# Casting double-precision weights on the chip: the last bit from a rounded sum in ScalarE, and a new fixed order of the first batch

## The chip, the core and the metric

The kernel runs on one core of a Trainium2 chip. The core has five engines with a queue of instructions each: TensorE (PE, with its weight loads shown as PEld), VectorE (DVE), ScalarE (ACT), GpSimd (POOL), and SyncE (SP), which here issues the loads. Each queue is worked off in order; semaphores hold an instruction until what it needs is there. The metric is device time in microseconds (us), lower is better.

## The reference

Two blocks in a row. The first is a gated linear attention (4 batches, 8 heads, 768 tokens, 48 channels a head); the second takes its output as a 768 x 384 matrix for each batch, mixes it with a two-dimensional Fourier transform, normalises it, and sends it through two projections with a residual.

```python
f = 1.0 / (1.0 + np.exp(-f_logit))
for t in range(S):
    state = f[:, :, t, :, None] * state + np.einsum('bhd,bhe->bhde', k[:, :, t], v[:, :, t])
    y[:, :, t] = np.einsum('bhd,bhde->bhe', q[:, :, t], state)
...
x = y.transpose(0, 2, 1, 3).reshape(B, S, H * D)
u = x + np.real(np.fft.fft(np.fft.fft(x, axis=1), axis=2))
un = (u - mean(u)) / np.sqrt(var(u) + 1e-06)
out = u + np.maximum(un @ w_ch1, 0.0) @ w_ch2
```

The two weight matrices (384 x 1536 and 1536 x 384) come as 64-bit floats. The kernel turns them into 32-bit floats on the chip: 24 blocks of 128 x 384 values.

## The kernel before, in words

A **unit** is one pair of heads of one batch; there are 16, four for each batch, numbered 0 to 15. `attention` (with `outputs`) is a generator: each `yield` ends a stage of a unit. Its stages, by the tiles they write: the gate's logarithm in `g` (a clamp on DVE, two activations on ACT); its running sum by a scan on DVE (L188), then two exponentials on ACT into `W` and `g`; two products on DVE (`W`, `q`; L199, L200), behind which the loads of f and k for unit u + 3 are issued, into the same buffers; the scores `sc` on PE (L210), masked into `at` by DVE (L214); the transposed keys `st`, copied to `kT` by ACT; the state's updates `ds` on PE, chained by a DVE scan into `stt`; the outputs `y` on PE in two sets (L381, L388); `yT`; the transpose `yt`; and its copy into `x` on ACT. `fold` then adds and subtracts halves of `x` for the Fourier transform (`eo`, `xs`, `xc`).

`fnet` is the second block for one batch: three groups of matmuls `z` (L461) with copies `zz`; the matmuls `mix` (L474), added to `x` by DVE; mean and variance by DVE (`bs`, `mv`) and two small activations (`rstd`); then, for each half of the 768 tokens, the normalised rows `un` (DVE), their transposes `pt` (PE) and copies `unT` (ACT), 12 groups of `up` (L516, w_ch1, each copied to `h` by ACT with a Relu), and three groups of `po` (L528, w_ch2), each over 12 blocks of `w2`.

A weight block is converted by `single`. The 64-bit words land in `raw` (two buffers of 384 KB), as a low and a high word for each value. DVE builds the sign, exponent and mantissa from the high word (L151, L152) and the low one (L153), takes the bit to round by (L155), POOL adds it (L156), and DVE multiplies small values to zero (L157) by a size that ACT took (L149). `weights(n)` converts what is missing of the first n blocks, ahead of the matmul that reads them.

The order of the first batch is written out by hand: the block under `manual_schedule` calls `step(u)` (one stage of a unit), `fill()` (one stage of `fnet`) and `weights(n)`. The program then goes on in the loop behind it, and there a scheduler orders the instructions of each engine.

Of the kernel before, what the change touches and what calls it, by code (L numbers as in the profile page):

```python
# [16 lines left out]
SMALLEST = 1.125 * 2.0 ** -15  # L17
X_MIN = -24.0
# [3 lines left out]
def kernel(  # L22
# [30 lines left out]
    pr = ctx.enter_context(tc.tile_pool(name="pr", bufs=2))  # L53
    p3 = ctx.enter_context(tc.tile_pool(name="p3", bufs=4))
    ph1 = ctx.enter_context(tc.tile_pool(name="ph1", bufs=14))
# [24 lines left out]
    masks = fixed([128, 4, 32], "masks")  # L80
    ident = fixed([128, 128], "ident")
    eps = fixed([128, 1], "eps")

    place = const.tile([128, B, 3], U32, tag="place", name="place")
    nc.gpsimd.iota(place, pattern=[[S, B], [-C, 3]], base=S, channel_multiplier=-1)
    nc.gpsimd.iota(place[0:1, :, 0], pattern=[[S, B]], base=HS, channel_multiplier=0)

    for i, t in enumerate(g_t):  # L90
        nc.gpsimd.memset(t[32:64], 30.0)
    for i in range(4):
        for t in k_t[i:i + 1] + q_t[i:i + 1]:
            nc.vector.memset(t[32:64], 0.0)
    nc.gpsimd.memset(bound, HIGH)
    nc.gpsimd.memset(bound.rearrange("p (c t) -> p c t", t=C)[:, :, 0:1], LOW)
    nc.gpsimd.memset(low, LOW)
    nc.gpsimd.memset(causal, 1.0)
    nc.gpsimd.affine_select(out=causal, in_=causal, pattern=[[1, C]], compare_op=ALU.is_ge, fill=0.0,
                            base=0, channel_multiplier=-1)  # L100
# [28 lines left out]
    nc.gpsimd.memset(eps, 1e-6)  # L129

    def zeros():
        for t in at_t + te_t:
# [4 lines left out]
    def single(dst, src):  # L137


        n = dst.shape[-1]  # L140
        raw = pr.tile([128, n, 2], U32, tag="raw", name="raw")
        nc.sync.dma_start(out=raw.rearrange("p n w -> p (n w)"), in_=src)
        lo, hi = raw[:, :, 0], raw[:, :, 1]
        size = ph1.tile([128, n], F32, tag="h1", name="size")
        half = ph1.tile([128, n], U32, tag="h1", name="half")
        bits = dst.bitcast(U32)
# [13 lines left out]
    blocks_of = [(w1[:, kt], w_ch1[kt * 128:(kt + 1) * 128], slice(o, o + 384))  # L160
                 for o in range(0, DFF, 384) for kt in range(3)]
    blocks_of += [(w2[:, m], w_ch2[m * 128:(m + 1) * 128], slice(0, DM)) for m in range(NF)]

    def weights(upto):
        while len(blocks_of) > 2 * NF - upto:
            dst, src, cols = blocks_of.pop(0)
            if src.dtype == F32:
                nc.sync.dma_start(out=dst[:, cols], in_=src[:, cols])
            else:
                single(dst[:, cols], src.bitcast(U32)[:, 2 * cols.start:2 * cols.stop])  # L170

    def attention(u, x_all):
# [17 lines left out]
        nc.gpsimd.tensor_copy(T[:, NCH - 1:], g[:, S - 1:S])  # L190
# [218 lines left out]
    def fold(u, x):  # L409
# [13 lines left out]
        if hp < HP // 2:  # L423
            return
# [259 lines left out]
```

## Time and profile before

| | us |
|---|---|
| median of 3 runs (667.94 to 670.15) | 670.06 |
| the profiled execution | 670.38 |
| its span, first to last instruction | 668.7 |
| PE busy in the span | 588.0 (88%) |
| DVE, ACT, POOL busy | 241.9, 170.5, 80.7 |

Busy PE time is not PE at its peak: matmuls overlap, and some run at a lower clock. The stages matter more than the shares: the weights are converted in the first third of the span, and the share of DVE is an average over a first third in which it works almost without a pause and a rest in which it hardly works.

### The profile page before, as it was taken

To read this page: it belongs to the slowest core of one execution; us is meant where nothing else is said; L and a number is where in the kernel's file an instruction comes from. 1 tells how busy PE (TensorE), PEld (TensorE's weight loads), DVE (VectorE), ACT (ScalarE), POOL (GpSimd) and SP (SyncE) were. 2 spreads that over 40 slices of the span, in tenths; PEclk is the share of its full clock that TensorE was granted. 3 is DMA by queue.
4 is the path that set the end of the run, shared out by engine and by line. 5 is a ranking of instruction groups with operands and counts; after the bars stand their busy time and mean duration, and the time that the engine had idled before them with its cause. 6 is when DMAs were issued, how large, how long until landed. Compare 5 with 4: busy or idle time off the path is not lost.

```text
span 668.7 us, 8382 instructions
## 1 busy us (share of the span) xinstructions
PE 588.0 (88%) x3458; PEld 365.1 (55%) x3458; DVE 241.9 (36%) x442; ACT 170.5 (26%) x317; POOL 80.7 (12%) x122
## 2 busy tenths in 40 slices
PE   0885938787888999989999999999999987999995
PEld 0764625455554655555556666656666544555552
DVE  6864768788988200430011033501011015000000
ACT  4542316445243310122023021420131011201200
POOL 4031111333332001200001010100001100000001
PEclk9986967889899999979999999999999987999998
DMA  8954031455453000000000110000000000000000
GB/s 197 266 145 119 24 120 46 132 143 154 141 157 110 30 1 24 13 26 1 24 22 0 30 42 1 1 1 13 24 1 1 24 12 1 0 13 24 0 13 29
DMA packets 15135, 35.50 MB, mean 53 GB/s; under 512 B 2608, under 2 KB 4656, under 8 KB 14960
## 3 DMA queue, kind: packets, MB, share of 16 engines
q1 hardware_dynamic: 14320, 32.52, 17.3%
q0 software_dynamic: 768, 2.36, 1.0%
q8 instruction: 29, 0.48, 0.3%
q14 instruction: 18, 0.15, 0.1%
HBM read 30.15 MB, written 4.72 MB: 52 GB/s over the span
## 4 chain that ended last, share of the span: by engine, by line
PE 73%; DVE 12%; ACT 4%; issue 4%; POOL 4%; DMA 2%; SPq 0%; ACTq 0%; POOLq 0%; DVEq 0%
PE up L516 28%; PE po L528 26%; PE z L461 5%; PE mix L474 3%; PE y L381 2%; POOL w L156 2%; DVE g L188 2%; PE y L388 2%; DMA g<-in_qkf_dram 2%; PE sc L210 1%; PE yt L400 1%; PE pt L508 1%; DVE bs L492 1%; DVE at L214 1%; DVE w L157 1%
## 5 line engine op out<-in xcount | busy, mean ns | idle before, releaser
L516 PE MATMUL up<-unT,w 128*128 128x384 f32 x576 | 200.2, 507 | 8.0 <-DVE w L157 6.6
L528 PE MATMUL po<-w,h 128*128 128x384 f32 x576 | 192.9, 492 | 8.9 <-DVE w L157 8.6
L516 PEld LDWEIGHTS up<-unT,w 128*128 128x128 f32 x576 | 111.6, 197 | 89.2 <-DVE w L157 9.9
L528 PEld LDWEIGHTS po<-w,h 128*128 128x128 f32 x576 | 108.3, 191 | 83.5 <-DVE w L157 10.6
L530 DVE TENSOR_TENSOR x<-po,x 128x384 f32<-128x384 f32 x24 | 13.3, 557 | 256.2 <-PE po L528 256.2
L519 ACT ACTIVATE h<-up 128x384 f32<-128x384 f32 x96 | 47.0, 490 | 151.7 <-PE up L516 151.6
L210 PE MATMUL sc<-q,W 48*64 48x128 f32 x768 | 34.7, 289 | 17.1 <-DVE q L200 16.7
L214 DVE COPY_PREDICATED at<-causal,sc 128x768 f32<-128x768 uint32 x32 | 32.0, 1027 | 46.4 <-PE sc L210 46.4
L419 POOL TENSOR_TENSOR eo<-x 128x288 f32<-128x288 f32 x12 | 14.3, 1188 | 214.9 <-ACT x L401 214.9
L210 PEld LDWEIGHTS sc<-q,W 48*64 48x64 f32 x768 | 26.3, 141 | 24.5 <-DVE q L200 16.7
L437 POOL DMA_INDIRECT out_dram<-x,place x12 | 11.9, 989 | 220.0 <-DVE x L530 213.3
L156 POOL TENSOR_TENSOR w<-w,half 128x384 uint32<-128x384 uint32 x24 | 26.6, 1114 | 57.6 <-DVE w L153 28.3
L509 ACT COPY unT<-pt 128x384 f32<-128x384 f32 x24 | 11.1, 479 | 81.9 <-PE pt L508 81.8
L381 PE MATMUL y<-at,v 128*64 128x128 f32 (+1 forms) x384 | 31.5, 301 | 0.0
L188 DVE TENSOR_TENSOR_SCAN g<-g,bound 112x768 f32<-112x768 f32 x16 | 28.8, 1805 | 0.4
L381 PEld LDWEIGHTS y<-at,v 128*64 128x64 f32 (+1 forms) x384 | 24.4, 142 | 6.2 <-issue 4.6
L388 PE MATMUL y<-q,stt 48*48 48x128 f32 x320 | 24.1, 285 | 1.5 <-DVE deep L187 1.4
L461 PE MATMUL z<-tab,xc 128*128 128x386 f32 (+1 forms) x64 | 20.0, 470 | 6.0 <-POOL xc L431 3.0
L474 PE MATMUL mix<-cd,zz 128*128 128x385 f32 x72 | 25.3, 495 | 0.0
L508 PE MATMUL pt<-ident,un 128*128 128x128 f32 x72 | 13.8, 319 | 12.2 <-DVE un L505 6.1
L388 PEld LDWEIGHTS y<-q,stt 48*48 48x48 f32 x320 | 19.3, 161 | 8.4 <-issue 5.2
L393 ACT COPY yT<-y 112x385 f32<-112x385 f32 x16 | 7.6, 477 | 58.0 <-PE y L388 57.9
(80 smaller groups left out, 478.5 us busy)
## 6 DMA issues: line engine op xcount, KB each, us to landing
raw<-in_w_ch_dram SPq DMA_DIRECT2D x24, 384.0 KB, 3.5
g<-in_qkf_dram SPq DMA_DIRECT2D x32, 144.0 KB, 3.9
k<-in_qkf_dram SPq DMA_DIRECT2D x32, 144.0 KB, 3.9
q<-in_qkf_dram SPq DMA_DIRECT2D x32, 144.0 KB, 3.6
v<-in_v_dram SPq DMA_DIRECT2D x16, 288.0 KB, 3.4
out_dram<-x SPq DMA_DIRECT2D x12, 192.0 KB, 1.9
tab<-in_seq_tab_dram SPq DMA_DIRECT2D x1, 1158.0 KB, 8.9
cd<-in_dim_tab_dram SPq DMA_DIRECT2D x1, 576.0 KB, 11.1
```

What stands on the lines that cost most here:

```text
L156: nc.gpsimd.tensor_tensor(bits, bits, half, ALU.add)
L188: nc.vector.tensor_tensor_scan(g, g, bound[:R], 0.0, ALU.add, ALU.min)
L210: nc.tensor.matmul(ps[64 * s:64 * s + 64, r, i * C:(i + 1) * C], lhsT=W[ROWS[r], o + 64 * s:o + 64 * s + 64], rhs=Q[ROWS[r], o:o + C], sta ...
L214: nc.vector.copy_predicated(AT[:, :, half], causal.bitcast(U32).unsqueeze(1).unsqueeze(1).to_broadcast([128, 2, NCH // 2, C]), ps[:, :, :N ...
L381: nc.tensor.matmul(y[FILL[r], c * C:(c + 1) * C], lhsT=vt[:, c, r * D:r * D + (64 if r == 0 else D)], rhs=AT[:, r, c], start=(c % 4 == 0), ...
L388: nc.tensor.matmul(y[ROWS[r], c * C:(c + 1) * C], lhsT=st[ROWS[r], :, c - 1], rhs=Q[ROWS[r], c * C:(c + 1) * C], start=False, stop=True, s ...
L461: nc.tensor.matmul(o, lhsT=lhsT, rhs=rhs, start=(i == 0), stop=(i == len(parts) - 1), skip_group_check=True)
L474: nc.tensor.matmul(mix[:rows.stop - rows.start, :n], lhsT=zz[:, T, rows], rhs=cd[:, T, :n], start=(T == 0), stop=(T == terms - 1))
L508: nc.tensor.transpose(pt[:, kt * 128:(kt + 1) * 128], un[:, kt * 128:(kt + 1) * 128], ident)
L516: nc.tensor.matmul(pp[:, :3 * 128], lhsT=w1[:, kt, m * 128:(m + 1) * 128], rhs=unT[:, kt], start=(kt == 0), stop=(kt == 2))
L519: nc.scalar.activation(h, pp[:, :3 * 128], AF.Relu)
L528: nc.tensor.matmul(po[:, :DM], lhsT=h1[m][:, i * 128:(i + 1) * 128], rhs=w2[:, m], start=(m == 0), stop=(m == NF - 1))
```

## The change

In `single`, three of DVE's five operations on a block go (the low word's OR, the rounding bit, the product that zeroes small values). In their place ACT adds 2^23 to the low word scaled by 2^-29, which rounds it, and takes 2^23 away again; POOL adds the result, as before. ACT also sums up, for each block, whether any value is too small; only then does the branch at the end of the program, which is not taken for these inputs, convert the weights in the old way and compute everything again. `raw` has three buffers for two, blocks are fetched as soon as a buffer is free, and `weights` in `fnet` runs four blocks further ahead.

```diff
-    pr = ctx.enter_context(tc.tile_pool(name="pr", bufs=2))
+    pr = ctx.enter_context(tc.tile_pool(name="pr", bufs=3))
...
     def first_loads():
-        load(0, "f", "k", "q")
+        load(0, "f")
+        load(1, "f")
+        load(0, "k", "q")
         nc.sync.dma_start(out=ident, in_=ident_in)
         load(0, "v")
-        for u in (1, 2):
-            load(u, "f", "k", "q", "v")
-        load(3, "q", "v")
...
+    def upper(dst, hi):
+        bits = dst.bitcast(U32)
+        nc.vector.tensor_scalar(bits, hi, 3, 0x3FFFFFF8, ALU.logical_shift_left, ALU.bitwise_and)
+        nc.vector.scalar_tensor_tensor(bits, hi, 0xC0000000, bits, ALU.bitwise_and, ALU.bitwise_or)
+        return bits
+
+    def single(i, dst, raw):
         lo, hi = raw[:, :, 0], raw[:, :, 1]
-        nc.scalar.activation(size, hi.bitcast(F32), AF.Abs)
-        vec.tensor_scalar(bits, hi, 3, 0x3FFFFFF8, ALU.logical_shift_left, ALU.bitwise_and)
-        vec.scalar_tensor_tensor(bits, hi, 0xC0000000, bits, ALU.bitwise_and, ALU.bitwise_or)
-        vec.scalar_tensor_tensor(bits, lo, 29, bits, ALU.logical_shift_right, ALU.bitwise_or)
-        vec.tensor_scalar(half, lo, 28, 1, ALU.logical_shift_right, ALU.bitwise_and)
-        nc.gpsimd.tensor_tensor(bits, bits, half, ALU.add)
-        vec.scalar_tensor_tensor(dst, size, SMALLEST, dst, ALU.is_ge, ALU.mult)
+        step = lo.bitcast(F32)
+        nc.scalar.activation(step, lo, AF.Identity, scale=2.0 ** -29, bias=whole)
+        nc.scalar.activation(lo, step, AF.Copy, bias=-WHOLE)
+        bits = upper(dst, hi)
+        nc.gpsimd.tensor_tensor(bits, bits, lo, ALU.add)
+        nc.scalar.activation(size, hi.bitcast(F32), AF.Abs)
+        nc.scalar.activation(size, size, AF.Relu, scale=-1.0, bias=least, accum_out=small[:, i:i + 1])
...
+                single(i, dst, raws[i])
+                fetch()
...
-        other = nc.vector if hp == HP - 1 else nc.gpsimd
+        last = hp == HP - 1
+        other = nc.vector if last else nc.gpsimd
         other.tensor_tensor(o[:, :, ch], x[:, 0:3, ch], x[:, 3:6, ch], ALU.subtract)
+        if last:
+            nc.vector.tensor_tensor(xs[:, :, lo:hi], o[:, :, lo:hi], o[:, :, up], ALU.subtract)
         nc.vector.tensor_tensor(e[:, 0:3, ch], x[:, 0:3, ch], x[:, 3:6, ch], ALU.add)
-        nc.gpsimd.tensor_copy(e[:, 3, ch], e[:, 0, ch])
+        other.tensor_copy(e[:, 3, ch], e[:, 0, ch])
...
-        for T in range(3):
+        for T in (2, 0, 1):
             z = ps_f.tile([128, 512], F32, tag="f", name=f"z{b}_{T}")
...
         for c in range(3):
             mix = mixed(f"mix{b}_{c}", slice(c * 128, (c + 1) * 128), DM + 1)
             nc.vector.tensor_tensor(x[:, c], mix[:, :DM], x[:, c], ALU.add)
+            moments(c)
+            deviation(slice(c, c + 1))
             nc.vector.tensor_tensor(x[:, c + 3], mix[:, DM:0:-1], x[:, c + 3], ALU.add)
             if c == 0:
                 nc.vector.tensor_copy(x[0:1, 3], row[0:1])
+            else:
+                turn(c - 1)
             yield
...
-                weights(m // 3 * 3 + 3)
+                weights(m // 3 * 3 + 3 + AHEAD)
...
-                    weights(NF + m + 1)
+                    weights(NF + m + 1 + AHEAD)
...
     with tc.manual_schedule():
+        start()
         first_loads()
-        for k in range(-1, HP):
-            for age in (-1, 0, 1, 2, 1, 0, 1, 2, 1):
-                if k - age < HP:
-                    step(k - age)
-            if k == -1:
-                zeros()
-            if k == 0:
+        step(0)
+        gap(k_t[1], q_t[1])
+        load(1, "k", "q", "v")
+        step(1)
+        for _ in range(3):
+            step(0)
+        zeros()
+        for k in range(1, HP):
+            if k == 1:
+                gap(k_t[2], q_t[2])
+                load(2, "f", "k", "q", "v")
+            if k == 2:
+                gap(q_t[3])
+                load(3, "q", "v")
+                fetch(3)
+            if k == 3:
                 tables()
+            for age in (-1, 0, 1, 2, 0, 1, 0):
+                step(k - age)
+            if k > 1:
+                weights(k - 1)
+            for age in (1, 2, 2, 1):
+                step(k - age)
+        step(4), step(3), step(2), step(3), step(2)
+        weights(3)
+        step(3), step(2), step(3)
+        step(4), step(3), step(4), step(3), step(3)
...
+        fill()
+        weights(4)
+        step(5), step(4)
+        fill()
+        weights(5)
...
+        weights(7)
```

`moments` is the mean and variance of one chunk of 128 tokens (DVE), `deviation` its two small activations, `turn` the rows `un`, their transposes `pt` and copy `unT` for one chunk; before, all six chunks had their moments behind the last `mix`.

What this does to the order of three queues follows, the program before first and the changed one second. **SP, the first loads.** g holds f; the buffers g_83, g_84, g_85 belong to units 0, 1 and 2, and then to 3, 4 and 5.

```order
L111 DMA v_138<-in_v_dram 128x576
L115 DMA g_84<-in_qkf_dram 48x768 x2
L115 DMA k_87<-in_qkf_dram 48x768 x2
L115 DMA q_90<-in_qkf_dram 48x768 x2
L111 DMA v_146<-in_v_dram 128x576
L115 DMA g_85<-in_qkf_dram 48x768 x2
L115 DMA k_88<-in_qkf_dram 48x768 x2
```

```order
L121 DMA v_140<-in_v_dram 128x576
L125 DMA k_87<-in_qkf_dram 48x768 x2
L125 DMA q_90<-in_qkf_dram 48x768 x2
L121 DMA v_152<-in_v_dram 128x576
L125 DMA g_83<-in_qkf_dram 48x768 x2
L125 DMA k_86<-in_qkf_dram 48x768 x2
L125 DMA g_85<-in_qkf_dram 48x768 x2
L125 DMA k_88<-in_qkf_dram 48x768 x2
```

The f of unit 1 moved to the front; the f of unit 2 (g_85) now stands behind the f and k of unit 3 (g_83, k_86), which go into buffers that unit 0 has to give up first.

**DVE, from the last mix of batch 0 to its rows un.** x_160 and x_142 are the same tile, batch 0's.

```order
L485 TENSOR_TENSOR x_160<-mix_2_809,x_160 128x384
L486 TENSOR_TENSOR x_160<-mix_2_809,x_160 128x384
L151 TENSOR_SCALAR w_103<-raw 128x384
L152 SCALAR_TENSOR_TENSOR w_103<-raw,w_103 128x384
L153 SCALAR_TENSOR_TENSOR w_103<-raw,w_103 128x384
L155 TENSOR_SCALAR half<-raw 128x384
L157 SCALAR_TENSOR_TENSOR w_103<-size,w_103 128x384
L214 COPY_PREDICATED at_94<-causal,sc_0_826 128x2x384
L214 COPY_PREDICATED at_94<-causal,sc_1_840 128x2x384
L492 BN_STATS bs_0_854<-x_160 128x6
L493 BN_AGGR mv_752<-bs_0_854 128x2
```

```order
L544 TENSOR_SCALAR un_0_842<-x_142,mv_793,rstd_794 128x384
L553 TENSOR_TENSOR x_142<-mix_2_857,x_142 128x384
L533 BN_STATS bs_2_862<-x_142 128x6
L534 BN_AGGR mv_793<-bs_2_862 128x2
L556 TENSOR_TENSOR x_142<-mix_2_857,x_142 128x384
L544 TENSOR_SCALAR un_1_868<-x_142,mv_793,rstd_794 128x384
L544 TENSOR_SCALAR un_2_875<-x_142,mv_793,rstd_794 128x384
L469 TENSOR_TENSOR eo_882<-x_402 128x3x96
```

A weight block, two masks and five further chunks' moments stood between the last mix and the rows; now one chunk's moments do.

**The conversions in batch 0's projections.** Before, on DVE, among the second matrix's blocks (w_104):

```order
L151 TENSOR_SCALAR w_104<-raw 128x384
L155 TENSOR_SCALAR half<-raw 128x384
L152 SCALAR_TENSOR_TENSOR w_104<-raw,w_104 128x384
L200 TENSOR_TENSOR q_91<-q_91,g_84 112x768
L153 SCALAR_TENSOR_TENSOR w_104<-raw,w_104 128x384
L151 TENSOR_SCALAR w_104<-raw 128x384
L214 COPY_PREDICATED at_94<-causal,sc_1_1846 128x2x384
L157 SCALAR_TENSOR_TENSOR w_104<-size,w_104 128x384
```

Now, on ACT, where the copies h of the up groups stand between them:

```order
L161 ACTIVATE raw_989<-raw_989,whole 128x384
L166 ACTIVATE size<-raw_989 128x384
L162 ACTIVATE raw_989<-raw_989 128x384
L581 ACTIVATE h_0_0_4_1016<-up_0_4_1012 128x384
L167 ACTIVATE size,small<-size,least 128x384
L161 ACTIVATE raw_1031<-raw_1031,whole 128x384
```

Before, attention's work and five operations a block took turns on DVE; now DVE has L151 and L152 of a block, and four activations of it stand on ACT. Seven blocks are converted ahead of batch 0's first up, for three before, and the attention of unit 6 and later stands behind the last block on DVE and ACT.

## Rows read from the trace of the kernel before

**Rows 1.** The page, busy tenths of PE and DVE in 40 slices of 16.7 us.
```profile
PE   0885938787888999989999999999999987999995
...
DVE  6864768788988200430011033501011015000000
```

**Rows 2.** Busy time of each engine by stage (from:to, length, busy us).
```profile
62.35:85.50 23.15, 23.15 (x179) 14.38 (x179) 14.50 (x27) 8.13 (x14) 3.27 (x5) 0.94 0.21 67
85.50:106.95 21.45, 8.49 (x97) 6.53 (x96) 16.59 (x38) 8.25 (x16) 1.99 (x4) 0.59 0.24 70
106.95:167.80 60.85, 49.27 (x409) 30.53 (x408) 50.31 (x89) 29.79 (x53) 20.56 (x23) 0.92 0.47 133
167.80:211.07 43.27, 37.01 (x325) 22.79 (x325) 39.66 (x75) 14.79 (x26) 13.29 (x14) 0.96 0.46 138
211.07:660.14 449.07, 437.18 (x1943) 262.83 (x1944) 76.08 (x155) 81.46 (x168) 25.01 (x37) 0.98 0.04 15
```

**Rows 3.** Groups by shape from 85 to 211 us: the conversion's instructions.
```profile
L156 POOL TENSOR_TENSOR w<-w,half 128x384 uint32<-128x384 uint32 x22 | 24.6, 1125 | 46.4 <-DVE w L153 28.3 <-DVE half L155 16.6 <-DVE deep L187 1.5
L157 DVE SCALAR_TENSOR_TENSOR w<-size,w 128x384 f32<-128x384 f32 x22 | 12.5, 570 | 10.0 <-POOL w L156 8.5 <-ACT size L149 1.3
L153 DVE SCALAR_TENSOR_TENSOR w<-raw,w 128x384 uint32<-128x384 uint32 x22 | 12.2, 556 | 0.1
L149 ACT ACTIVATE size<-raw 128x384 f32<-128x384 f32 x22 | 12.1, 555 | 21.7 <-POOL w L156 15.8 <-DMA raw<-in_w_ch_dram 5.9
L155 DVE TENSOR_SCALAR half<-raw 128x384 uint32<-128x384 uint32 x22 | 7.6, 355 | 0.0
```

**Rows 4.** The chain that ended last: fnet's parts on PE (start us, us).
```profile
221.49 23.42 PE up L516 x72
244.91 23.22 PE po L528 x72
268.13 8.14 PE z L461 x28
...
277.01 6.04 PE mix L474 x18
```

**Rows 5.** The chain again: a unit's parts on PE, and two transposes pt.
```profile
66.02 1.47 PE sc L210 x48
...
71.73 0.63 PE st L351 x5
...
74.32 0.71 PE ds L360 x18
75.28 1.45 PE y L381 x23
...
79.61 1.27 PE y L388 x20
...
83.02 0.59 PE yt L400 x6
...
219.79 0.94 PE pt L508 x6
```

**Rows 6.** Timelines of SP and DVE in the head, and landing of that load.
```profile
9.56 1.31 SPq L115 DMA_DIRECT2D g<-in_qkf_dram  x2
...
g<-in_qkf_dram SPq DMA_DIRECT2D x2, 144.0 KB, 6.2
...
11.35 0.56 DVE L180 TENSOR_SCALAR g<-g 112x768 f32<-112x768 f32 x1 [2.66 <-DMA g<-in_qkf_dram]
...
17.28 1.76 DVE L188 TENSOR_TENSOR_SCAN g<-g,bound 112x768 f32<-112x768 f32 x1
```

**Rows 7.** The chain before the first projection.
```profile
85.94 5.38 issue
```

**Rows 8.** DMA issues from 117 to 211 us: count, size, median us to landing.
```profile
raw<-in_w_ch_dram SPq DMA_DIRECT2D x19, 384.0 KB, 3.4
```

**Rows 9.** Timeline of PE: the last batch's transposes.
```profile
559.34 0.97 PE L508 MATMUL pt<-ident,un 128*128 128x128 f32 x6 [3.63 <-DVE mv L493]
```

More of the change, by code (lines that the diff above doesn't have):

```diff
@@ L79, with gap, start @@
     cd = fixed([128, 3, DM + 1], "cd")
-    masks = fixed([128, 4, 32], "masks")
     ident = fixed([128, 128], "ident")
     eps = fixed([128, 1], "eps")
+    whole = fixed([128, 1], "whole")
+    least = fixed([128, 1], "least")
+    size = fixed([128, 384], "size")
+    small = fixed([128, 2 * NF], "small")
     place = const.tile([128, B, 3], U32, tag="place", name="place")
[L85 to L93, printed above, removed]
-            nc.vector.memset(t[32:64], 0.0)
[L95 to L100, printed above, removed]
+    def gap(*tiles):
+        for t in tiles:
+            nc.vector.memset(t[32:64], 0.0)
+    def start():
+        for t in g_t:
+            nc.gpsimd.memset(t[32:64], 30.0)
+        gap(k_t[0], q_t[0])
+        nc.gpsimd.memset(bound, HIGH)
+        nc.gpsimd.memset(bound.rearrange("p (c t) -> p c t", t=C)[:, :, 0:1], LOW)
+        nc.gpsimd.memset(low, LOW)
+        nc.gpsimd.memset(eps, 1e-6)
+        nc.gpsimd.memset(whole, WHOLE)
+        nc.gpsimd.memset(least, SMALLEST)
+        for t in te_t:
+            nc.gpsimd.memset(t, 0.0)
+        nc.gpsimd.memset(causal, 1.0)
+        nc.gpsimd.affine_select(out=causal, in_=causal, pattern=[[1, C]], compare_op=ALU.is_ge, fill=0.0,
+                                base=0, channel_multiplier=-1)
     v_of = {}
@@ L135, in zeros @@
         nc.gpsimd.memset(xs[:, :, 0:1], 0.0)
[L137 to L142, printed above, removed]
-        lo, hi = raw[:, :, 0], raw[:, :, 1]
-        size = ph1.tile([128, n], F32, tag="h1", name="size")
-        half = ph1.tile([128, n], U32, tag="h1", name="half")
-        bits = dst.bitcast(U32)
+        nc.gpsimd.memset(small, 0.0)
+        nc.gpsimd.iota(place, pattern=[[S, B], [-C, 3]], base=S, channel_multiplier=-1)
@@ L162, with words @@
     blocks_of += [(w2[:, m], w_ch2[m * 128:(m + 1) * 128], slice(0, DM)) for m in range(NF)]
-    def weights(upto):
[L165 to L168, printed above, removed]
-            else:
-                single(dst[:, cols], src.bitcast(U32)[:, 2 * cols.start:2 * cols.stop])
+    wide = w_ch1.dtype != F32
+    raws, done = [], [0]
+    def words(i):
+        _, src, cols = blocks_of[i]
+        raw = pr.tile([128, 384, 2], U32, tag="raw", name=f"raw{i}")
+        nc.sync.dma_start(out=raw.rearrange("p n w -> p (n w)"),
+                          in_=src.bitcast(U32)[:, 2 * cols.start:2 * cols.stop])
+        return raw
@@ new lines, in fetch @@
+    def fetch(n=1):
+        for _ in range(n):
+            if wide and len(raws) < len(blocks_of):
+                raws.append(words(len(raws)))
+    def weights(upto):
+        while done[0] < min(upto, len(blocks_of)):
+            i = done[0]
+            dst, src, cols = blocks_of[i]
+            if wide:
+                if len(raws) <= i:
+                    fetch()
+                single(i, dst, raws[i])
+                fetch()
+            else:
+                nc.sync.dma_start(out=dst, in_=src[:, cols])
+            done[0] += 1
@@ L488, in fnet @@
                 nc.vector.tensor_copy(x[0:1, 3], row[0:1])
+            else:
+                turn(c - 1)
             yield
[L490 to L497 removed]
+        turn(2)
         yield
         for half in range(2):
[L501 to L510 removed]
+            if half:
+                for c in range(3, NCH):
+                    moments(c)
+                deviation(slice(3, NCH))
+                unT = p2.tile([128, 3, 3 * 128], F32, tag="unT", name=f"unT{b}_1")
+                for c in range(3, NCH):
+                    turn(c)
             h1 = []
             for m in range(NF):
[L513 removed]
+                weights(m // 3 * 3 + 3 + AHEAD)
                 pp = ps_f.tile([128, 512], F32, tag="f", name=f"up{b}_{half}_{m}")
@@ L582 @@
         fill()
-        weights(3)
-        step(5)
-        fill()
+        step(4)
+        fill(), fill()
+        step(4), step(5)
         step(6)
+        weights(7)
     tc.no_sync_barrier()
@@ L604 @@
     with tc.If(again > 0):
-        nc.sync.dma_start(out=masks, in_=sel)
+        if wide:
+            for i, (dst, _, _) in enumerate(blocks_of):
+                single_or_zero(dst, words(i))
+        nc.sync.dma_start(out=size.rearrange("p (i n) -> p i n", n=32)[:, 0:4], in_=sel)
         for u in range(4):
```

88 lines of the change are left out of this document (47 added, 41 removed).

## The prediction

> **What bounds the kernel now.** I read the page's busy tenths first [rows 1]: DVE is at 7 to 9 up to the 13th slice (some 215 us) and nearly idle behind it, while PE is at 9 almost without a break from there on. So there are two regimes, and a list of the stages shows them [rows 2]: up to 211.07 us, where the first half of batch 0's projections is nearly done, DVE is busy 50.31 of 60.85 us and 39.66 of 43.27; from 211.07 to 660.14 PE is busy 437.18 of 449.07 us.
>
> Busy PE hides slow PE, so I count PE's work at the pace it has when nothing holds it. An up of half a batch takes 23.42 us, its po 23.22, a batch's z 8.14 and its mix 6.04 [rows 4]; a unit's six parts 1.47 + 0.63 + 0.71 + 1.45 + 1.27 + 0.59 = 6.12, and two transposes pt 0.94 [rows 5]. Over the program: 8 up (187.4), 8 po (185.8), 4 z (32.6), 4 mix (24.2), 24 pt (11.3), 16 units (97.9): 539 us. The span is 668.7 us, so 130 us are lost to waits and slow matmuls. Where: at the first up (106.95 us) PE has done units 0 to 4 (30.6), of unit 5 sc, st, ds and part of y (3.4), and batch 0's z, mix and three pt (15.6): 49.6, so 57 us are lost by then. At 211.07 it has done units 0 to 8, most of 9 and half of 10 (63.5), z, mix and pt (15.6), an up (23.4) and two po groups (15.5): 118. So 36 us are lost between the two, 28 between 211.07 and 660.14 (449.07 less the 421 that are left), and 8.6 behind PE's last po. A gain must come from the 93 us of the first 211.
>
> Why are they lost? Between first and last conversion DVE does five operations a block and attention's work in one queue. The groups by shape [rows 3] give 0.57 us for L157, 0.556 for L153 (L152 is its like), 0.355 for L155 (L151 is its like): 2.4 us of DVE a block, and DVE waits 8.5 us for POOL besides, in front of L157. The last twelve blocks take 43.27 us [rows 2], 3.6 each, when attention's work shares the queue. PE needs 1.95 us a block of the first matrix (23.42/12), and two po steps a block of the second (23.22/36 x 2 = 1.3). So DVE sets the pace.
>
> **The change, part by part.**
>
> *Conversion.* DVE loses L157, L153 and L155, 1.48 us a block, 36 us in all; 0.9 us stay. ACT goes from one activation to four. The trace has no such Identity, Copy or Relu with a sum; the nearest row is L149, 0.555 us on the same shape [rows 3]. Below, nothing suggests less than that; above, an extra read of the sum may add as much as another L149. I take 4 x 0.555 = 2.2 us a block. POOL's addition stays at 1.125 us. Then the ring of buffers: a block's low word is free after two or three activations (1.67) and POOL (1.125), and the next lands 3.4 us after its issue [rows 8]: 6.2 us, with three buffers 2.07 a block. On ACT the copies h stand between, one for each block of the first matrix, at about 0.55. So a block takes between 2.07 (the ring alone) and 2.8 (four activations and a copy); I take 2.35, nearer to the ring, since a copy is there only for some blocks. The upper bound is that nothing is won: 3.6.
>
> The Trainium skill speaks against this move ("ScalarE: Activation LUTs", Rules for kernel authors): adds, products and Relu belong on VectorE. The same page's section on what ACT_TABLE_LOAD costs gives 186 ns + 0.833 ns an element, some 93 ns more for a bias from memory, and 93 ns of overlap between neighbours. An estimate by it is 1.84 us a block, under the ring's 2.07, and 19 blocks would be 5 us sooner than I say. By the rows its rule on engines is right as a price (1.67 us more on ACT for 1.48 less on DVE) and beside the point while DVE is the engine that is late.
>
> *Head, up to the first z (62.35 us).* The f of unit 1 moves ahead, which takes away the 2.66 us for which DVE waited in front of its clamp [rows 6], and five of seven memsets leave DVE's start. Unit 0's products should then end near 11.3 us (f landed at some 4.5, clamp, two activations, scan, two activations, product). But the f of unit 2 now stands behind loads into unit 0's buffers, so it is issued near 13.2 instead of 9.56; with 6.2 us to land at the worst and half of that at the best [rows 6] it is there at 16.5 to 19.5. Its clamp stands in DVE's queue ahead of unit 1's scan, which began at 17.28 [rows 6] and will begin at about 17.7. So what the head wins is lost again there. Behind it, the order has ACT copy unit 0's yT ahead of unit 2's exponentials, and each of three early blocks puts 0.9 us on DVE and 2.2 on ACT ahead of a unit's work: 2 us later by unit 3. Against that, unit 4's scan and products no longer wait behind its late clamp and load, and unit 4's scores are done ahead of z. Walking the queues, the first z starts near 57, with unit 4's sc behind it. Bounds: 53, and 65 if the load of unit 2's f is at its worst and the blocks delay each unit.
>
> *From z to the first up (44.6 us before).* Here PE lost most: 8.49 of 21.45 us busy from 85.5 on [rows 2]. The cause is in the order of DVE: a weight block, two masks and six moments ahead of the rows un, with 5.38 us for the block's data [rows 7]. Now one chunk's moments stand there, and five blocks are done before. The work is z 8.14, mix 6.04, unit 4's rest 4.65, pt 1.4, unit 5's sc and st 2.1, and a row of small matmuls 0.7: 23. To that I add waits: about 2 us where unit 4's kT stands on ACT behind four activations of a block, 2 us at the first pt (its rows come behind the second mix's additions), 2 at the second, under 1 for the rest. So the first up starts at 57 + 30 = 87, with 48.3 us of work done: 39 lost where it was 57.
>
> *Batch 0's projections.* Five blocks are there at 87; the other 19 take 19 x 2.35 = 45 us, to 132, and POOL 1.1. The up groups need 12 blocks and take 23.4 + 3.4 us with unit 5's parts, so they end near 114 and hardly wait. The po groups wait for blocks: the last po_0 step comes at 133 to 134, and nine steps (5.8 us) follow, to 140. Work: 23.4 + 15.5 + 3.4 = 42.3 in 53 us, 11 lost where it was 36.
>
> *The rest.* 539 - 48.3 - 42.3 = 448.5 us of work is left, for 421 before: units 6 to 10, which before filled PE's waits for weights, come now in the full stretch. The 28 us lost there may grow: each unit's DVE and ACT chain stands in it, and before batch 1's first z the order has PE take half of unit 9's scores, whose product stands on DVE behind xs (2 to 3 us). They may shrink in the last batch: z begins with xs alone, and the wait of 3.63 us in front of its transposes [rows 9] is cut into pieces, though three more moments still stand ahead of its third rows un. I take 31, between 25 and 45. The end stays at 8.5; a reduction and a maximum more are done long before.
>
> *Sum.* 140 + 448.5 + 31 + 8.5 = 628 us of span, 41 less than 668.7. The profiled time was 670.38, 1.7 over its span; the median of the runs, 670.06, is 0.3 below that. So **630 us**, 6% less.
>
> **The rivals.**
>
> *ACT becomes what DVE was* (weights remain the pace). For it: four activations a block, waiting in a strict queue for data, with the copies h behind them; a waiting activation holds up the h that frees PE's buffer. At 3.6 us a block, 19 blocks end 24 us later than I say: 652 to 656. Against: the two longest rows, the ring and ACT, are both under 2.9.
>
> *Faster on every edge:* the first up at 82, blocks at 2.07, later losses 25: 140 - 10 + 448.5 + 25 + 8.5, some 612 of span, 614.
>
> *The gain goes to later stalls:* attention that filled PE's waits comes where it must be on time, and 45 us or more are lost there, 645 to 667. For it: seven units and two transitions in the tight stretch; against: from 211.07 on PE lost only 28 of 449 us with five units in it [rows 2].
>
> *Slower:* one mechanism, ACT held by late loads. The weights' ring and all other loads share SP's queue, and each issue waits for what stands ahead (a load of v waits for a unit's y on PE). If that makes a block take over 4.4 us, the projections end past 180 and the time is 670 or more; at 5 us it is 680. Against: the queue has three blocks of lead, and landing takes 3.4 us.
>
> **How the numbers follow.** The forecast (615 to 645) 0.72; ACT as the pace (645 to 657) 0.12; better still (under 615) 0.05; the gain lost to later stalls (645 to 667) 0.05, of which 0.01 comes within 0.5%; other ways to no change 0.02; slower 0.04. About 0.5% is what a measurement can tell from no change. The range, 613 to 654, leaves out the slow case, no change, and parts of the other edges. Faster by over 0.5% has 0.72 + 0.12 + 0.05 + 0.04 = 0.93, within 0.5% 0.03, slower 0.04.
>
> **What would show it.** In the trace after: the first up near 87 us and the last of batch 0's po_1 near 140; from one block's POOL addition to the next, 2.1 to 2.8 us; the clamp of unit 2 waiting for its load at 13 to 18 us; PE at 9 from the ninth slice on. I am wrong if activations on the raw words take much over 0.6 us, if PE waits in the up groups for ACT's h, or if the stretch behind 140 loses over 45 us.

## The result, and the profile after

The changed kernel takes 642.77 us (median of 4 runs, 642.26 to 644.33) against 669.49 for the kernel before beside it: a ratio of 0.9608, interval 0.9583 to 0.9633. Forecast were 630 us, 613 to 654. The profiled execution has a span of 641.0 us.

The page's busy tenths of PE and DVE, in slices of 16.0 us, answer to [rows 1]:

```profile
PE   1578964999899999999999999999999887999994
...
DVE  5777556658411357522300138100200132000000
```

From the eighth slice (112 us) to the 33rd PE is at 8 or 9; before, slices 7 to 13 (up to 217 us) were at 7 or 8. DVE's long stretch of 5 to 8 ends with the tenth slice. The stages (from:to, length, busy us of PE, PEld, DVE, ACT, POOL, granted clock) answer to [rows 2]. The cuts are the first z, the first up, the end of po_1 and the last po, behind which the span's last 8.60 us lie:

```profile
64.60:96.18 31.58, 25.37 (x195) 16.15 (x192) 17.80 (x34) 14.25 (x31) 3.48 (x6) 0.94 0.25 71
96.18:151.55 55.37, 45.85 (x190) 26.20 (x189) 34.16 (x65) 51.73 (x122) 21.20 (x21) 0.91 0.47 139
151.55:632.40 480.85, 464.44 (x2522) 287.84 (x2520) 116.96 (x219) 109.35 (x220) 28.14 (x43) 0.99 0.08 24
```

| stretch | before | forecast | measured |
|---|---|---|---|
| start to the first z | 62.35 | 57 | 64.60 |
| first z to first up | 44.60 | 30 | 31.58 |
| first up to end of po_1 | stage cut otherwise | 53 | 55.37 |
| from there to the last po | stage cut otherwise | 448.5 + 31 | 480.85 |
| behind the last po | 8.6 | 8.5 | 8.60 |

The forecast's stretches add up to 628, the measured ones to 641. Of the 13 us between them 7.6 lie ahead of the first z, 1.6 behind it, 2.4 in batch 0's projections, 1.4 in the rest.

The groups by shape from 96 to 152 us show what a block costs now and what PE waits for (they answer to [rows 3]):

```profile
L578 PE MATMUL up<-unT,w 128*128 128x384 f32 x72 | 26.2, 521 | 8.5 <-ACT h L581 8.5
L164 POOL TENSOR_TENSOR w<-w,raw 128x384 uint32<-128x384 uint32 x19 | 20.6, 1087 | 28.0 <-ACT raw L162 23.0 <-DVE w L152 3.4 <-DVE w L151 0.9
L590 PE MATMUL po<-w,h 128*128 128x384 f32 x48 | 16.3, 496 | 1.0 <-POOL w L164 1.0
...
L152 DVE SCALAR_TENSOR_TENSOR w<-raw,w 128x384 uint32<-128x384 uint32 x19 | 12.7, 672 | 0.5
L161 ACT ACTIVATE raw<-raw,whole 128x384 f32<-128x384 uint32 x19 | 12.2, 645 | 1.6 <-DVE w L152 1.6
L167 ACT ACTIVATE size<-size,least 128x384 f32<-128x384 f32 x19 | 11.8, 618 | 0.1
L162 ACT ACTIVATE raw<-raw 128x384 uint32<-128x384 f32 x19 | 10.6, 558 | 0.1
L166 ACT ACTIVATE size<-raw 128x384 f32<-128x384 f32 x19 | 10.4, 547 | 0.0
...
L151 DVE TENSOR_SCALAR w<-raw 128x384 uint32<-128x384 uint32 x19 | 8.2, 433 | 19.1 <-DMA raw<-in_w_ch_dram 19.1
...
L167 ACT ACTIVATION_READ_ACCUMULATOR size<-size,least 128x1 f32 x19 | 3.8, 202 | 0.0
```

The po groups hardly wait any more (1.0 us). The up groups wait once, 8.5 us, for ACT's copy h; the timeline of PE has the place:

```profile
96.18 4.05 PE L578 MATMUL up<-unT,w 128*128 128x384 f32 x12
108.76 6.11 PE L578 MATMUL up<-unT,w 128*128 128x384 f32 x12 [8.53 <-ACT h L581]
```

In those microseconds ACT worked off the conversions of four blocks and began a fifth; the first h stands behind them (L161 and L162 round the low word, L166 and L167 check the size):

```profile
98.62 0.64 ACT L161 ACTIVATE raw<-raw,whole 128x384 f32<-128x384 uint32 x1
99.29 0.55 ACT L162 ACTIVATE raw<-raw 128x384 uint32<-128x384 f32 x1
...
100.92 0.61 ACT L161 ACTIVATE raw<-raw,whole 128x384 f32<-128x384 uint32 x1
...
103.19 0.61 ACT L161 ACTIVATE raw<-raw,whole 128x384 f32<-128x384 uint32 x1
103.71 0.52 ACT L166 ACTIVATE size<-raw 128x384 f32<-128x384 f32 x1
...
105.70 0.62 ACT L161 ACTIVATE raw<-raw,whole 128x384 f32<-128x384 uint32 x1
...
107.72 0.62 ACT L161 ACTIVATE raw<-raw,whole 128x384 f32<-128x384 uint32 x1
108.25 0.46 ACT L581 ACTIVATE h<-up 128x384 f32<-128x384 f32 x1
```

From one block to the next ACT takes 2.30, 2.27, 2.51 (a copy kT of 0.60 us stands in it) and 2.02 us. DVE meanwhile stood 5.21 us for a block's data: the loads into the three raw buffers had been issued by 75.04 us, and SP could issue the next load only at 100.96, when the first of them was given up (timelines of DVE and SP):

```profile
104.18 0.36 DVE L151 TENSOR_SCALAR w<-raw 128x384 uint32<-128x384 uint32 x1 [5.21 <-DMA raw<-in_w_ch_dram]
...
100.96 19.07 SPq L190 DMA_DIRECT2D raw<-in_w_ch_dram  x8
```

In the head, the f of unit 2 is issued at 13.94 (9.56 before), DVE's clamp waits for it, and unit 1's scan starts at 18.90 in place of 17.28 [rows 6] (timelines of SP and DVE):

```profile
13.94 0.89 SPq L125 DMA_DIRECT2D g<-in_qkf_dram  x2
...
18.23 0.56 DVE L220 TENSOR_SCALAR g<-g 112x768 f32<-112x768 f32 x1 [4.37 <-DMA g<-in_qkf_dram]
...
18.90 1.76 DVE L228 TENSOR_TENSOR_SCAN g<-g,bound 112x768 f32<-112x768 f32 x1
```

### The profile page after: what moved, and what is told of

Its sections match the earlier page's. It is cut to its first block, busy times and chain, and to the rows that moved or that the text cites. A ratio compares the mean times of both kernels' runs of the same rounds, so it can differ in the third digit from the quotient of the medians.

```text
span 641.0 us, 8416 instructions
## 1 busy us (share of the span) xinstructions
PE 573.2 (89%) x3458; PEld 362.2 (57%) x3458; DVE 215.5 (34%) x386; ACT 209.9 (33%) x429; POOL 73.4 (11%) x113
## 4 chain that ended last, share of the span: by engine, by line
PE 59%; DVE 3%; ACT 1%; issue 0%; POOL 0%; DVEq 0%
PE up L578 22%; PE po L590 22%; PE z L508 4%; PE mix L521 2%; PE y L424 2%; PE y L431 1%; PE sc L252 1%; PE pt L547 1%; PE yt L443 1%; PE ds L403 1%; DVE at L256 1%; DVE bs L533 0%; PE st L394 0%; DVE un L544 0%; DVE x L553 0%
## 5 line engine op out<-in xcount | busy, mean ns | idle before, releaser
L578 PE MATMUL up<-unT,w 128*128 128x384 f32 x576 | 194.6, 497 | 9.7 <-ACT h L581 8.5
L590 PE MATMUL po<-w,h 128*128 128x384 f32 x576 | 190.0, 489 | 1.0 <-POOL w L164 1.0
L252 PE MATMUL sc<-q,W 48*64 48x128 f32 x768 | 32.5, 296 | 13.5 <-DVE q L242 12.2
L256 DVE COPY_PREDICATED at<-causal,sc 128x768 f32<-128x768 uint32 x32 | 31.6, 1028 | 31.5 <-PE sc L252 31.5
L164 POOL TENSOR_TENSOR w<-w,raw 128x384 uint32<-128x384 uint32 x24 | 25.9, 1079 | 56.2 <-ACT raw L162 51.2
L424 PE MATMUL y<-at,v 128*48 128x128 f32 (+1 forms) x384 | 31.4, 302 | 0.0
L424 PEld LDWEIGHTS y<-at,v 128*48 128x48 f32 (+1 forms) x384 | 25.1, 144 | 5.5 <-issue 4.5
L521 PE MATMUL mix<-cd,zz 128*128 128x385 f32 x72 | 27.3, 520 | 0.0
L221 ACT ACTIVATE g<-g 112x768 f32<-112x768 f32 x16 | 13.6, 847 | 35.3 <-DVE g L220 35.3
L412 DVE TENSOR_TENSOR_SCAN stt<-ds,te 112x288 f32<-112x288 f32 x16 | 12.0, 750 | 31.8 <-PE ds L409 31.8
L241 DVE TENSOR_TENSOR W<-W,k 112x768 f32<-112x768 f32 x16 | 15.7, 984 | 16.8 <-ACT W L234 15.8
```

Of the source, the lines that this page charges most:

```text
L164: nc.gpsimd.tensor_tensor(bits, bits, lo, ALU.add)
L241: nc.vector.tensor_tensor(W, W, K, ALU.mult)
L252: nc.tensor.matmul(ps[64 * s:64 * s + 64, r, i * C:(i + 1) * C], lhsT=W[ROWS[r], o + 64 * s:o + 64 * s + 64], rhs=Q[ROWS[r], o:o + C], sta ...
L256: nc.vector.copy_predicated(AT[:, :, half], causal.bitcast(U32).unsqueeze(1).unsqueeze(1).to_broadcast([128, 2, NCH // 2, C]), ps[:, :, :N ...
L424: nc.tensor.matmul(y[FILL[r], c * C:(c + 1) * C], lhsT=vt[:, c, r * D:r * D + (64 if r == 0 else D)], rhs=AT[:, r, c], start=(c % 4 == 0), ...
L521: nc.tensor.matmul(mix[:rows.stop - rows.start, :n], lhsT=zz[:, T, rows], rhs=cd[:, T, :n], start=(T == 0), stop=(T == terms - 1))
```

## The experiments

My theory was the forecast's: the gain comes from taking operations off DVE, which set the pace. The rival: it comes from the new order of the first batch, with more blocks converted ahead of the first up. (Seven stand ahead of it in the written order. In the trace five are done by then, for three before; blocks 5 and 6, counted from 0, have their first activations at 98.62 and 100.92 us, behind the first up at 96.18.) A third part of the change, the third raw buffer, proved to need runs of its own.

### Conversion, buffer and order, apart

**old_conversion**: the changed program, each block converted by the old recipe.

```diff
-                single(i, dst, raws[i])
+                single_or_zero(dst, raws[i])
```

Expected: 

> The changed program in every order, load and buffer, but each block's weights are converted by the kernel before's recipe (one Abs on ScalarE, five operations on VectorE, one add on GpSimd; small weights made zero at once). Theory (the gain comes from taking half of the conversion off VectorE): VectorE is the pace of the projections again; some 19 blocks at 2 more operations of 0.56 to 0.57 us each and one more in place of none put back 25 to 33 us less what lies in VectorE's idle time, so the time goes back to 657 to 672 us, and po's matmuls wait for VectorE or GpSimd again. Rival (the new order of the first batch, blocks 1 to 7 converted before the first up matmul, gives the gain): 641 to 648 us, no wait in po's groups.

**new_conversion**: the kernel before, with the changed `single`.

```diff
-        vec.scalar_tensor_tensor(bits, lo, 29, bits, ALU.logical_shift_right, ALU.bitwise_or)
-        vec.tensor_scalar(half, lo, 28, 1, ALU.logical_shift_right, ALU.bitwise_and)
-        nc.gpsimd.tensor_tensor(bits, bits, half, ALU.add)
-        vec.scalar_tensor_tensor(dst, size, SMALLEST, dst, ALU.is_ge, ALU.mult)
+        nc.scalar.activation(step, lo, AF.Identity, scale=2.0 ** -29, bias=whole)
+        nc.scalar.activation(lo, step, AF.Copy, bias=-2.0 ** 23)
+        nc.gpsimd.tensor_tensor(bits, bits, lo, ALU.add)
+        nc.scalar.activation(size, size, AF.Relu, scale=-1.0, bias=least, accum_out=small[:, i:i + 1])
```

Expected: 

> The kernel before in its own order, with two raw buffers and no blocks further ahead; only the conversion of a block is the changed one (four ScalarE activations, two VectorE operations, one GpSimd add; the sum that detects small weights is computed and not read, and small weights are not made zero). Theory: po's groups lose their 23 us waits for the most part, 645 to 656 us, of the 27 us gained some 14 to 24 are there without the order. Rival (order gives it): 663 to 670 us. A third outcome, worse than before, would say that ScalarE's activations placed in the old order hold up the first batch's own ScalarE work.

**new_ring3**: new_conversion with a third raw buffer (`pr` with bufs=3; to make room, the size tile is one for all and a ring of tiles that attention uses too, `ph1`, has 13 buffers for 14).

Expected: 

> The kernel before's order with the changed conversion, as in new_conversion, and a third raw buffer. There the blocks followed each other at some 3.6 us (GpSimd's adds from 117.1 to 182.7 us), against 2.5 us in the changed program. Theory (with two buffers the landing of 3.3 us and the conversion take turns, and the third buffer sets the pace): 2.4 to 2.7 us a block, the first batch's projections 18 to 24 us shorter, 628 to 636 us. Rival (the pace comes from blocks fetched and converted four ahead, in an order in which ScalarE does not wait on h): 645 to 652 us.

**ring3_only**: the kernel before with the third buffer; its own conversion stays. To make room, the size tile is one for all, the half word is written into the raw tile, and `ph1` has 13 buffers for 14; these were not tried by themselves.

Expected: 

> The kernel before in its own order and with its own conversion, and only a third raw buffer (the half word is written into the raw tile, the size tile is one for all). GpSimd's adds followed each other there at 4.46 us (117.6 to 206.8 us, 20 steps). Theory (VectorE's five operations are the pace, as the forecast had it): a third buffer frees nothing, 664 to 671 us. Rival (with two buffers a block's landing of 3.4 us and its conversion take turns, and that is the pace): 2.8 to 3.8 us a block, 645 to 658 us.

**ring2_new**: the changed program with two.

```diff
-    pr = ctx.enter_context(tc.tile_pool(name="pr", bufs=3))
+    pr = ctx.enter_context(tc.tile_pool(name="pr", bufs=2))
...
-                fetch(3)
+                fetch(2)
```

Expected: 

> The changed program with two raw buffers in place of three (and two blocks fetched first in place of three). If the third buffer is worth in this order what it was worth in the order of before (651.4 to 642.2 us), the blocks come at some 3.5 us, up and po wait for GpSimd's adds, 650 to 656 us. If blocks four ahead make up for it, 642 to 646 us.

Measured (medians of 4 runs; ratio to the kernel before, which ran beside each at 669.5 to 670.1):

| order | conversion | raw buffers | kernel | us | ratio, interval |
|---|---|---|---|---|---|
| old | old | 2 | before | 669.49 | |
| old | old | 3 | ring3_only | 657.73 | 0.9809 (0.9786 to 0.9833) |
| old | new | 2 | new_conversion | 651.37 | 0.9739 (0.9710 to 0.9768) |
| old | new | 3 | new_ring3 | 642.18 | 0.9597 (0.9570 to 0.9624) |
| new | old | 3 | old_conversion | 651.56 | 0.9717 (0.9692 to 0.9741) |
| new | new | 2 | ring2_new | 647.75 | 0.9671 (0.9649 to 0.9694) |
| new | new | 3 | the changed kernel | 642.77 | 0.9608 (0.9583 to 0.9633) |

In the old order the conversion is worth 18 us, the third buffer 12, both together 27: all of what the change won. The new order adds nothing to the two together. Beside the old conversion it is worth 6 us (657.73 to 651.56), beside two buffers 3.6. So my theory's span held for new_conversion (645 to 656) and missed for old_conversion, which came out 5 us under 657 to 672; the rival's 641 to 648 for it is refuted too. new_ring3 and ring2_new came out between their two expectations: the third buffer is worth 9 us beside the new conversion in the old order, and 5 in the new.

For ring3_only my theory's 664 to 671 is refuted. The rival's numbers came true: 657.73 us, at the upper edge of its span, and 3.49 us from one block's addition on POOL to the next (106.06 to 175.87 us, 20 steps), for 4.46 before. Its reason, load and conversion taking turns, is not what the traces show. Over those 20 steps the stages (as in [rows 2]) are, for the kernel before and for ring3_only:

```profile
117.64:206.84 89.20, 72.68 (x659) 45.37 (x660) 77.66 (x145) 38.51 (x68) 29.95 (x33) 0.94 0.51 148
```

```profile
106.06:175.87 69.81, 58.41 (x339) 32.66 (x339) 62.16 (x121) 28.32 (x51) 30.61 (x26) 0.97 0.46 145
```

DVE was busy 87% of the time with two buffers and 89% with three, and of its waits with two hardly any is for raw data (us, times, longest):

```profile
DVE w L151 <- DMA raw<-in_w_ch_dram: 0.3, 1, 0.3
```

By its busy time DVE stayed the pace. What fell is its other work: attention's operations and the rest took 42 us of the longer stretch and 24 of the shorter (sums of the groups there; of the masks `at`, 10 and 4). With three buffers the scheduler put a part of that work behind the last block, where PE sets the pace. Why it did so is not shown. old_conversion fits this: DVE is busy 56.93 of 64.57 us between its additions (97.47 to 162.04). With the new conversion ACT takes its place: busy 57.81 of 65.64 us in new_conversion, 44.57 of 46.49 in new_ring3, 42.92 of 44.65 in the changed kernel.

PE's waits in batch 0's projections show the difference (us, times, longest), of ring3_only:

```profile
PE po L527 <- DVE w L155: 7.3, 7, 2.3
PE up L515 <- DVE w L155: 5.0, 4, 1.7
```

of new_conversion:

```profile
PE po L532 <- POOL w L160: 5.4, 7, 1.5
PE up L520 <- POOL w L160: 4.4, 4, 2.1
```

of old_conversion:

```profile
PE up L578 <- ACT h L581: 13.3, 4, 9.5
PE po L590 <- DVE w L178: 6.4, 5, 2.3
```

and of new_ring3:

```profile
PE po L532 <- POOL w L159: 2.6, 4, 1.0
PE up L520 <- POOL w L159: 0.7, 1, 0.7
```

With the old conversion PE waits for DVE, with two buffers for POOL's late addition, and only with both changed are the waits small. All three programs in the new order wait for h (8.5 us the changed kernel, 13.3 old_conversion, 11.3 ring2_new), those in the old order do not. This is where the new order's gain went. new_ring3's first up comes 7 us later (timeline of its PE), and from there it has no such stall, so that both begin the second half's up at about the same time, 170.57 and 170.45 us.

```profile
103.10 14.12 PE L520 MATMUL up<-unT,w 128*128 128x384 f32 x40
...
170.57 23.49 PE L520 MATMUL up<-unT,w 128*128 128x384 f32 x72
```

### The wait of 8.53 us for h

**blocks_ahead**: blocks 5 and 6 (counted from 0) are converted earlier in the hand-written order.

```diff
         step(5), step(4)
+        weights(6)
         fill()
         step(4)
         fill()
         step(4)
+        weights(7)
         fill(), fill()
         step(4), step(5)
         step(6)
-        weights(7)
```

Expected: 

> The changed program with the conversions of blocks 5 and 6 moved ahead into the fills before mix, in place of all up to block 6 after the first batch's last step before the up matmuls. TensorE waited 8.53 us at 108.76 us for ScalarE's h, which stood behind the activations of four blocks (98.6 to 108.3 us). Theory (queue order on ScalarE is the cost): the wait falls to 1 to 4 us, time 635 to 640 us. Rival (what comes late is GpSimd's adds or the raw data, and ScalarE's order only shows it): the wait moves to the weights of the up groups and the time stays within 1.5 us of 642.8.

**no_check**: two of the four activations go.

```diff
-        nc.scalar.activation(size, hi.bitcast(F32), AF.Abs)
-        nc.scalar.activation(size, size, AF.Relu, scale=-1.0, bias=least, accum_out=small[:, i:i + 1])
```

Expected: 

> The changed program without Abs and the summed Relu on ScalarE; the detection of small weights is left out. Two of a block's four activations go, 0.54 and 0.61 us and 0.19 for reading the sum, 1.34 us a block, 32 us of ScalarE's 210. If the up groups' 8.53 us wait for h is ScalarE's queue, four blocks there take 5.4 us less: the wait falls to 2 to 4 us, po's waits go, and the time is 634 to 639 us. If VectorE's or GpSimd's part or the raw data comes last in any case, it is 641 to 644 us.

**ahead0**: `AHEAD = 0` for 4.

Expected: 

> The changed program with blocks converted no further ahead than before inside the projections (0 in place of 4; seven are still converted before the first up). ScalarE then has blocks 5 and 6 in front of the first h, in place of 5 to 8 and a part of 9. Theory (the 8.53 us wait is made by conversions, and their wait for raw data, queued in front of h): the wait halves to 3 to 5 us; blocks then come later, and po or up waits for them 2 to 6 us; 638 to 643 us. Rival (four ahead is what hides the blocks): 645 to 652 us.

Measured: blocks_ahead 631.81 us (0.9446, 0.9417 to 0.9475), 11 us faster than the changed kernel and below the 635 to 640 expected. PE's timeline has two short waits in place of 8.53 us, and the twelve matmuls behind them take 4.4 us in place of 6.11:

```profile
95.44 4.05 PE L578 MATMUL up<-unT,w 128*128 128x384 f32 x12
100.35 2.20 PE L578 MATMUL up<-unT,w 128*128 128x384 f32 x6 [0.86 <-ACT h L581]
102.84 2.17 PE L578 MATMUL up<-unT,w 128*128 128x384 f32 x6 [0.29 <-ACT h L581]
```

no_check came out at 642.64 (0.9599, 0.9577 to 0.9622): no gain, against my 634 to 639, and within the 641 to 644 of its other case. PE still waited 8.22 us for h. ACT now waits for a block's data where it worked before, and h stands behind that (timeline of its ACT):

```profile
102.81 0.64 ACT L161 ACTIVATE raw<-raw,whole 128x384 f32<-128x384 uint32 x1 [2.69 <-DMA raw<-in_w_ch_dram]
```

But the edit changed more than the two activations: the scheduler ordered the queues anew. In front of no_check's first h (108.20 us) stand five whole blocks and a unit's two exponentials (105.26 and 107.45 us); in the changed kernel it was four blocks and one activation of a fifth. From the first of the last 19 additions to the last, the stages are, for the changed kernel and for no_check:

```profile
99.92:144.57 44.65, 35.13 (x156) 20.23 (x156) 25.90 (x46) 42.92 (x107) 19.99 (x19) 0.89 0.52 155
```

```profile
98.54:146.35 47.81, 35.41 (x157) 19.72 (x155) 41.45 (x66) 35.15 (x67) 26.00 (x23) 0.93 0.54 169
```

DVE's busy time grew from 25.90 to 41.45 us, by attention's work that stood behind the last block before. So no_check shows neither that ACT's check is free nor that the raw data alone holds h.

ahead0 came out at 642.78 (0.9601, 0.9577 to 0.9625) with the same wait, 8.51 us. The time lies in the theory's span by luck, since the wait that was to halve did not change; the rival's 645 to 652 is refuted. The built order of ACT explains it: it is the same up to the first h. Behind the hand-written part a scheduler places the conversions, and it set the same four blocks in front of h whichever number the program asks for. blocks_ahead differs in two things, how many blocks the hand-written order has converted and how early their buffers are free for the next loads: it issues loads at 78.10 and 89.30 us for one at 100.96, and one block's activations begin in front of h. These two, fewer conversions in front of h and earlier data, were not tried apart.

### The head, and the order of the moments

**f2_ahead**: unit 2's f with the first loads.

```diff
         load(0, "v")
+        load(2, "f")
...
-                load(2, "f", "k", "q", "v")
+                load(2, "k", "q", "v")
```

Expected: 

> The changed program with one move: unit 2's decay load (f) is issued at the end of the first loads in place of behind unit 1's k, q, v. If the late decay (VectorE waited 4.37 us for it at 18.23 us) is what puts the first z at 64.6 us in place of the 57 predicted, z comes 3 to 5 us sooner and the time is 638 to 640 us. If the head is set by TensorE at its lower clock and by ScalarE's order behind it, z moves less than 1.5 us and the time is 641.5 to 644 us.

Measured: 638.64 us (0.9509, 0.9466 to 0.9552; runs from 633.62 to 640.38), in the span that was expected if the late load is the cost. The first z comes at 60.19 us, 4.4 sooner. In the profiled run, the longest of the four, the first up is only 2.0 sooner, since PE ran at a granted clock of 0.85 from there to the first up, for 0.94 in the changed kernel (timeline of PE):

```profile
60.19 3.65 PE L509 MATMUL z<-tab,xs 128*128 128x386 f32 x6
...
82.49 0.52 PE L548 MATMUL pt<-ident,un 128*128 128x128 f32 x3 [2.38 <-DVE un L545]
...
83.42 3.81 PE L522 MATMUL mix<-cd,zz 128*128 128x385 f32 x6
...
94.21 5.56 PE L579 MATMUL up<-unT,w 128*128 128x384 f32 x12
```

The same mix took 2.12 us in the changed kernel, behind the same wait of 2.38.

**old_moments**: the moments, deviations and first three turns behind the last mix, as before.

Expected: 

> The changed program, but with the moments of all six chunks, their deviations and the first three turns behind the last mix as in the kernel before (z stays in its new order). Theory from the forecast (in place of one wait of 4.54 and one of 1.21 us before, two waits of 2.4 us, and one half's moments moved behind the first half): each of the two ends of a Fourier part that no unit's work covers loses 0 to 3 us, 643 to 648 us. Rival (the moments' order is what brought the first up from 107 to 96 us): 650 us or more.

Measured: 639.39 us (0.9544, 0.9513 to 0.9576), 3.4 faster, where I expected 0 to 6 slower. The first up comes 1 us later (97.14), but in the last batch, where no unit's work lies between, the changed order has PE wait twice and run a mix at the lower clock (changed kernel, PE):

```profile
525.52 0.62 PE L547 MATMUL pt<-ident,un 128*128 128x128 f32 x3 [2.06 <-DVE mv L534]
525.94 3.73 PE L521 MATMUL mix<-cd,zz 128*128 128x385 f32 x6
...
533.15 0.90 PE L547 MATMUL pt<-ident,un 128*128 128x128 f32 x3 [3.15 <-DVE un L544]
```

for once in old_moments, as in [rows 9]:

```profile
528.69 0.97 PE L547 MATMUL pt<-ident,un 128*128 128x128 f32 x6 [3.63 <-DVE mv L534]
529.87 0.88 PE L547 MATMUL pt<-ident,un 128*128 128x128 f32 x3 [0.21 <-DVE un L544]
```

### The versions put together

**both_ahead** is f2_ahead and blocks_ahead in one. Expected: 

> The changed program with both moves: unit 2's decay loaded with the first loads, and the conversions of blocks 5 and 6 before mix's fills. Alone the one brought the first z from 64.6 to 60.2 us (but the first up only from 96.2 to 94.2, with TensorE at a lower clock between), the other the wait at the second up group from 8.53 to 1.15 us. Theory (the two losses are separate): 2 to 4 us below blocks_ahead's 631.8, so 627 to 631 us. Rival (what the earlier decay saves is waited again before the first up, or is lost to the clock): 631 to 634 us.

**first_moments** is both_ahead with the changed order of the moments in the first batch alone.

```diff
-            moments(c)
-            deviation(slice(c, c + 1))
+            if b == 0:
+                moments(c)
+                deviation(slice(c, c + 1))
...
```

Expected: 

> both_ahead, with the moments of the second to the last batch behind the last mix as in the kernel before, and only the first batch in the changed order. In old_moments the last batch went from z to its first up in 21.5 us, in the changed program in 24.5 (two waits, 2.06 and 3.15 us, and a lower clock after the first). So 3 us below both_ahead, 622 to 625 us; 626 to 629 if old_moments' gain was from the first batch or the half switches.

Measured: both_ahead 627.19 us (0.9369, 0.9345 to 0.9394), 4.6 below blocks_ahead, as expected if the two losses are separate. first_moments 625.57 (0.9345, 0.9323 to 0.9368; 5 runs), the fastest here and 17 us below the changed kernel; it lies between its two expectations, and its 1.6 below both_ahead lie within the two intervals, so what the moments are worth beside the other two stays open.

## Why the prediction was right, and where it was not

The sign, the mechanism for most of the gain and the range held. Point by point:

- **Conversion.** Taking work off DVE is worth 18 us alone and 9 (651.56 to 642.77) beside the rest. ACT's price was nearly right: 2.2 us a block forecast, 2.0 to 2.3 measured without other work between. From one block's addition to the next it was 2.48 us (99.92 to 144.57, 18 steps), for 2.35. I leaned to the ring of buffers as the pace; by its busy time (42.92 of 44.65 us) it was ACT. So the rival *ACT becomes what DVE was* names the mechanism, at 2.48 us a block and not at 3.6. By "ScalarE: Activation LUTs" of the Trainium skill (what ACT_TABLE_LOAD costs, and the formula there) my estimate was 1.84. The trace does not agree: four activations take 0.55 to 0.65 us each, the read of the sum is an instruction of 0.20 us more, and two neighbours overlap where the second does not read what the first wrote (0.52 us from the start of L161 to that of L166) and not where it does (0.67 us from L161 to L162). The page's rule against such work on ACT did not decide: new_conversion, which moves the work there, is 18 us faster.
- **"So DVE sets the pace"** held, as far as busy time shows it: DVE worked 87% of the time, and 0.3 us of its waits were for raw data. What the forecast did not ask is what else stands in DVE's queue between two blocks, and what a third raw buffer would give by itself: 12 us. Its 3.6 us a block, the upper bound and the rival's price, is the last twelve blocks' pace; over 20 steps it was 4.46. And its reading of DVE at 7 to 9 up to the 13th slice is too high for the first six, at 4 to 8; nothing hangs on that.
- **Head: the term that was mis-sized.** The first z was forecast at 57 us, with 65 as its bound, and came at 64.6. The load of unit 2's f landed within the times forecast (16.5 to 19.5; the clamp ran at 18.23), but this cost more behind it than I walked through the queues: 4.4 of the 7.6 us go when that load is moved. The other 3 were not taken apart; PE's granted clock of 0.90 there is one candidate, argued only.
- **From z to the first up**: 31.6 us for 30, and the two waits at pt of 2.38 us each were forecast as 2 and 2. This gain was real, and new_ring3, without it, is as fast: it was lost in the next stage.
- **Batch 0's projections.** The sum was nearly right (55.4 us for 53), but its make-up was not, so that is luck. "They end near 114 and hardly wait" failed: the last up ended at 133, PE waited 8.53 us for h, the sign that I had named for being wrong, and po's wait, where I had put the loss, was 1.0. This is what the rival *ACT becomes what DVE was* said, in small: ACT's queue, holding h behind conversions. The forecast counted the five blocks that are done at the first up, and not the four that stand between it and the first h.
- **The rest**: 31 us lost forecast, 480.85 - 448.5 = 32.4 measured. That the wait at the last transposes would be "cut into pieces" held, and the pieces (2.06 and 3.15 us) cost more than the whole (3.63).

## What to carry to other kernels

When an engine looks like the pace of a pipeline, ask what else stands in its queue between the operations that you count, and try the ring of buffers that feeds it by itself: here a third buffer was worth 12 us and the lighter conversion 18. The shorter path to the first up added nothing to these two, since the first copy that frees PE stood behind conversions in ACT's queue. So count what stands in front of the first consumer's instruction on every queue when that consumer comes earlier. And where a scheduler orders the queues, look at the built order of each run: in ring3_only and no_check it moved attention's work too, so neither shows the price of its one edit.

## What the runs showed of the hardware

- A summed activation leaves a second instruction on ACT, 0.20 us each (x19), which the forecast had only as an upper bound.
- The same six matmuls of mix, behind the same wait of 2.38 us, took 2.12 us in one program and 3.81 in another: TensorE's two clock levels, with granted clocks of 0.94 and 0.85 over the stretch. Which of the two comes I could not tell from what PE did just before.
- L152 took 0.672 us on average in the projections, for 0.556 of its like before [rows 3]. The mean hides two cases: sixteen took 0.52 to 0.56 us, and three 1.26, 1.26 and 1.41. Each of the three began while an addition of POOL ran, and ended 0.42 us behind it; one pair (timelines of POOL and DVE):

```profile
127.73 1.22 POOL L164 TENSOR_TENSOR w<-w,raw 128x384 uint32<-128x384 uint32 x1 [0.74 <-DMA raw<-in_w_ch_dram]
...
128.11 1.26 DVE L152 SCALAR_TENSOR_TENSOR w<-raw,w 128x384 uint32<-128x384 uint32 x1
```
